# Strided attention heads: a multiplicative mask on GpSimd in place of mask products on TensorE

## The chip, the cores and the metric

The kernel runs on one core of a Trainium2 chip. Its metric is the device time of one execution, in microseconds, as the median of repeated runs. A core has five engines with a queue each: TensorE (PE in the profile; PEld is its weight load), VectorE (DVE), ScalarE (ACT), GpSimd (POOL) and SyncE (SP), which here issues most DMAs. Each queue is worked off in its own order; semaphores tie the queues to one another.

## The reference

Attention with 8 batches, 8 heads, 576 positions and head size 64, in float32, followed by a mixture of experts with one expert per token. Heads 0 to 3 look back at most 31 positions (local), heads 4 to 7 at positions that are equal modulo 32 (strided):

```python
scores = scale * np.matmul(q, k.transpose(0, 1, 3, 2))
rel = pos[:, None] - pos[None, :]
mask_local = (rel >= 0) & (rel < stride)
mask_strided = (rel >= 0) & (pos[None, :] % stride == pos[:, None] % stride)
scores = np.where(masks[None, :, :, :], scores, -1000000000.0)
attn = np.exp(scores - np.max(scores, axis=-1, keepdims=True))
attn = attn / (np.sum(attn, axis=-1, keepdims=True) + 1e-09)
x = np.matmul(attn, v)          # heads are then joined to rows of 512
```

The mixture takes the gate logits of each row, picks an expert by the largest logit (or keeps the expert of the row before, where a second gate says so), and multiplies the row's softmax probability with `relu(x @ w1[e]) @ w2[e]`; 8 experts, 512 to 1024 to 512.

## The kernel before

**Tiling.** Heads are worked in pairs: per batch pairs 0 and 1 are local, pairs 2 and 3 strided, so a strided pair stands in steps 2 and 3 of every four. A pair consists of two units (`g` 0 and 1). For strided heads the positions are regrouped by their residue modulo 32: seven residues of 18 positions make a block of 126 (`GK`), and the last four residues a block of 72 (`GL`). A strided unit has two blocks of 126 (252 columns a head), or two of 126 and one of 72 (324 columns). Inside a block only positions of the same residue, and no later ones, may be seen, so the mask is the same for every block, `maskS`.

**One unit.** `scores` writes the scores, keys on partitions and queries along the row, into a PSUM tile (two of them), and ScalarE takes the exponential into a tile `e` in SBUF (four of them) without a maximum. For local units `mask` multiplies `e` by ones and zeros on VectorE (L263). For strided units `mask` does nothing: there `scores` first writes the mask into PSUM by a product of the identity with `maskS` (bfloat16, 0 or a large negative number; L246, one for each head), and the score products (L252) are added to it, so that the exponential of what must not be seen is zero. `values` (L276) multiplies `e` with the values, which have a column of ones at the end that yields the sums; `norm` divides by them (L289, L290) on VectorE. In the profile one float32 product of L252 or L276 stands as four records.

**The order of the work** is written out by hand, in program order for each engine, in the loop at the end of `attention`. Step n, out of 35, does in this order: the load of pair n+4 (L164, L168, by SP); scores and masks of pair n; the stores of pair n-2 (L301, L307, by SP: two DMAs for a batch's local half, ten for its strided half); the transpositions of pair n-2 (L317, copied out by ScalarE, L321); values and norm of pair n-1; two steps of the weight sums of expert 0 on VectorE from step 9 on (L703; the weights themselves are loaded in step 6); after a batch's last pair the gate logits (L336) and gates (L354 onward). Local pairs of batch 0 are steps 0 and 1, its strided pairs steps 2 and 3, those of batch 1 steps 6 and 7, and so on to 30 and 31.

**What hangs on the steps.** A table `also` puts the routing into them: in step 2 `router.constants` (a row of iotas on GpSimd, L478 to L504, that VectorE reads, and a DMA from GpSimd's queue, L505); in steps 19 to 23 the routing of the first four batches on VectorE and TensorE; in steps 24 to 33 two scatters each from GpSimd's queue (L577; each writes up to 128 entries of 8 bytes to a table of slots in DRAM); in step 29, behind its two scatters, two gathers from GpSimd (L737) of the rows of the first expert tile, whose row numbers VectorE makes late in that step (L632 to L637). Before the loop, GpSimd and VectorE make `maskL` (L185 to L190) and `maskS` (L195 to L215). After the loop the experts run, on TensorE mainly (L807, L843), with the routing of the last four batches, its twenty scatters and their fetch among their first products.

Of the kernel before, what the change touches and what calls it, by code (L numbers as in the profile page):

```python
# [8 lines left out]
F32 = mybir.dt.float32  # L9
BF16 = mybir.dt.bfloat16  # L10
I32 = mybir.dt.int32
Act = mybir.ActivationFunctionType
Alu = mybir.AluOpType
# [5 lines left out]
P = 128  # L19
B, H, S, DH = 8, 8, 576, 64  # L20
# [19 lines left out]
GK, GL = PL * GC, PL * GR  # L40
# [19 lines left out]
NEG = -8.0e9  # L60
# [17 lines left out]
def across(ap, shape):  # L78

    return ap.rearrange("a (o b) -> a o b", o=1).to_broadcast(shape)  # L80
# [62 lines left out]
def attention(ctx, tc, qkl, qks, vl, vs, wg, xd, ident, router, moe):  # L143

    nc = tc.nc
    sums, probs, codes = router.sums, router.probs, router.codes
    consts = ctx.enter_context(tc.tile_pool(name="consts", bufs=1))
# [27 lines left out]
    for _ in range(WARM):  # L175
        ps = psV.tile([P, 512], F32, name="vps")
# [1 line left out]
    wgs = consts.tile([P, DK, 32], F32, name="wgs")  # L178
    nc.scalar.dma_start(out=wgs, in_=wg.rearrange("(k p) e -> p k e", p=P))

    identb = consts.tile([P, P], BF16, name="identb")
    nc.vector.tensor_copy(identb, ident)

    maskL = consts.tile([LK, LT, LQ], F32, name="maskL")
    nc.gpsimd.memset(maskL, 1.0)  # L185
# [1 line left out]
                            pattern=[[0, LT], [-1, LQ]], channel_multiplier=1)  # L187
    nc.gpsimd.affine_select(out=maskL, in_=maskL, compare_op=Alu.is_ge, fill=0.0, base=STRIDE,
                            pattern=[[0, LT], [1, LQ]], channel_multiplier=-1)
    nc.gpsimd.memset(maskL[0:STRIDE, 0], 0.0)  # L190

    maskS = consts.tile([GK, 2 * GK + GL], BF16, name="maskS")
    for n, c in ((GK, GC), (GL, GR)):
        i = consts.tile([GK, n], I32, name=f"i{n}")
        cls = consts.tile([GK, n], F32, name=f"cls{n}")  # L195
        div = consts.tile([GK, n], F32, name=f"div{n}")
        both = []
        for mult, pattern in ((1, [[0, n]]), (0, [[1, n]])):

            nc.gpsimd.iota(i, pattern=pattern, base=0, channel_multiplier=mult)  # L200
            t = consts.tile([GK, n], F32, name=f"cls{n}{mult}")
            nc.vector.tensor_copy(t, i)
            nc.vector.tensor_scalar(i, i, 65536 // c + 1, None, Alu.mult)
            nc.vector.tensor_scalar(i, i, 16, None, Alu.arith_shift_right)
            nc.vector.tensor_copy(div, i)
            nc.vector.scalar_tensor_tensor(t, div, -float(c), t, Alu.mult, Alu.add)
            both.append(t)
        nc.vector.tensor_tensor(cls, both[0], both[1], op=Alu.not_equal)
        nc.vector.tensor_scalar(cls, cls, NEG, None, Alu.mult)
        nc.gpsimd.affine_select(out=cls, in_=cls, compare_op=Alu.is_ge, fill=NEG, base=0, pattern=[[1, n]],  # L210
                                channel_multiplier=-1)
        if n == GK:
            nc.vector.tensor_copy(maskS[:, 0:2 * n].rearrange("p (a x) -> p a x", a=2), across(cls, [n, 2, n]))
        else:
            nc.vector.tensor_copy(maskS[:, 2 * GK:], cls)  # L215
# [13 lines left out]
    start = consts.tile([P, CH], F32, name="start")  # L229
    nc.vector.tensor_scalar(start, pos8, float(E), None, Alu.is_equal)  # L230

    def spans(u):

        if u.local:
            return [(3 * u.g + i, LQ, i * LQ) for i in range(3)]
        return [(j, GK if j < GT - 1 else GL, i * GK) for i, j in enumerate(range(2 * u.g, 2 + 3 * u.g))]

    def scores(u):
        t = st["qk", u.b, u.pair]
        kb, width = (LK, LQ) if u.local else (GK, GK)  # L240
        ps = psS.tile([P, 2, 512], F32, name="sps")
        sp = spans(u)
        n = sp[-1][2] + sp[-1][1]
        if not u.local:
            for h in range(2):
                nc.tensor.matmul(ps[0:GK, h, 0:n], lhsT=identb[0:GK, 0:GK],  # L246
                                 rhs=maskS[:, 0:n], start=True, stop=False, skip_group_check=True)
        for j, w, c in sp:
            m = kb if u.local else w
            for h in range(2):  # L250
                r = slice(h * DH, (h + 1) * DH)
                nc.tensor.matmul(ps[0:m, h, c:c + w], lhsT=t[r, S + j * width:S + j * width + m],  # L252
                                 rhs=t[r, j * width:j * width + w],
                                 start=(u.local and c == 0), stop=True, skip_group_check=True)
        e = work.tile([P, 2, 2 * GK + GL], F32, name="e")
        nc.scalar.activation(e[0:kb, :, 0:n], ps[0:kb, :, 0:n], Act.Exp, bias=0.0, scale=1.0 / DH ** 0.5)  # L256
        u.e = e

    def mask(u):
        if u.local:  # L260
            ev = u.e[:, :, 0:3 * LQ]
            m = maskL[:, 3 * u.g:3 * u.g + 3].rearrange("p a x -> p (a x)")
            nc.vector.tensor_tensor(ev, ev, m.rearrange("p (o x) -> p o x", o=1).to_broadcast([LK, 2, 3 * LQ]),  # L263
                                    op=Alu.mult)

    def values(u):

# [130 lines left out]
    n = PAIRS * RB + 3  # L398
# [4 lines left out]
    m = n  # L403
# [10 lines left out]
    for n in range(len(units) + 3):  # L414
        if n < len(units):
            if n + ahead < len(order):
                load(*order[n + ahead])
            if n == 6:
                steps = moe.W[0].ready(nc, w1=moe.w1, w2=moe.w2, e=0)
            for u in units[n]:  # L420
                scores(u)
                mask(u)
# [1046 lines left out]
```

## Time and profile before

| | us |
|---|---|
| median of 13 runs (742.17 to 751.01) | 744.66 |
| profiled execution | 747.47 |
| its span, from first to last instruction | 745.7 |
| TensorE busy | 697.9 |
| VectorE busy | 380.6 |
| ScalarE busy | 199.1 |
| GpSimd busy | 134.3 |
| mean granted TensorE clock | 0.953 of full speed |

The attention stage fills the first 202 us; the first expert product (L807) starts at 201.9. In the profile a row of a timeline has the start in us, the duration in us, the engine, the line, the operation, `out<-in`, partitions x elements and type, a count, and in brackets how long the engine had idled and what ended that. "issue" is time in which an engine waited for nothing that the profile shows, and "remote" a release that it can't assign. A busy TensorE is not the same as one at its peak.

### The profile page before, as it was taken

To read this page: it belongs to the slowest core of one execution; us is meant where nothing else is said; L and a number is where in the kernel's file an instruction comes from. 1 tells how busy PE (TensorE), PEld (TensorE's weight loads), DVE (VectorE), ACT (ScalarE), POOL (GpSimd) and SP (SyncE) were. 2 spreads that over 40 slices of the span, in tenths; PEclk is the share of its full clock that TensorE was granted. 3 is DMA by queue.
4 is the path that set the end of the run, shared out by engine and by line. 5 is a ranking of instruction groups with operands and counts; after the bars stand their busy time and mean duration, and the time that the engine had idled before them with its cause. 6 is when DMAs were issued, how large, how long until landed. Compare 5 with 4: busy or idle time off the path is not lost.

```text
span 745.7 us, 15189 instructions
## 1 busy us (share of the span) xinstructions
PE 697.9 (94%) x6170; PEld 623.8 (84%) x6170; DVE 380.6 (51%) x896; ACT 199.1 (27%) x360; POOL 134.3 (18%) x150
## 2 busy tenths in 40 slices
PE   8999999497899599999999999999999999999993
PEld 5887888385699589899998899999999999989992
DVE  6568756272466434473563266366346646324341
ACT  2444443041321112222212222212222222212310
POOL 3000001405127331211121120131012112111001
PEclk8999999597699799999999999999999999999997
DMA  9898778342360023604322612520071342010100
GB/s 326 262 332 289 271 276 295 125 144 62 87 226 30 3 85 103 213 30 151 127 73 78 220 58 82 204 86 31 27 247 58 125 158 73 32 35 31 31 29 27
DMA packets 38057, 95.83 MB, mean 129 GB/s; under 512 B 5358, under 2 KB 14574, under 8 KB 37888
## 3 DMA queue, kind: packets, MB, share of 16 engines
q1 hardware_dynamic: 29616, 73.77, 28.4%
q0 software_dynamic: 7744, 20.08, 8.3%
q8 instruction: 64, 1.05, 0.6%
q14 instruction: 105, 0.86, 0.3%
q10 hardware_dynamic: 528, 0.07, 0.1%
HBM read 74.93 MB, written 20.02 MB: 127 GB/s over the span
## 4 chain that ended last, share of the span: by engine, by line
PE 88%; DVE 3%; another core or an unknown queue 3%; issue 2%; DMA 1%; ACT 1%; POOL 1%; POOLq 0%; ACTq 0%
PE lps L807 31%; PE mps L843 30%; PE vps L276 6%; PE sps L252 6%; PE tps L317 4%; PE xps L750 2%; PE lps L898 2%; PE mps L909 2%; PE sps L246 2%; PE vps L354 1%; PE tps L336 1%; DMA qk<-in_qks_dram 1%; DVE xl L290 1%; DMA x<-xd,gi 0%
## 5 line engine op out<-in xcount | busy, mean ns | idle before, releaser
L807 PE MATMUL lps<-tt,ws 128*128 128x128 f32 x912 | 108.5, 275 | 1.5 <-issue 1.5
L807 PEld LDWEIGHTS lps<-tt,ws 128*128 128x128 f32 x912 | 105.0, 192 | 1.6 <-issue 1.6
L763 POOL DMA_INDIRECT out_dram<-y,tab x40 | 45.9, 1146 | 330.9 <-DVE y L795 274.5
L843 PE MATMUL mps<-wt,k 128*128 128x256 f32 x456 | 101.6, 379 | 0.0
L843 PEld LDWEIGHTS mps<-wt,k 128*128 128x128 f32 x456 | 86.6, 190 | 11.8
L795 DVE TENSOR_TENSOR h<-lps,u 128x512 f32<-128x512 f32 x57 | 39.4, 691 | 81.1 <-PE lps L807 71.0
L807 PE MATMUL lps<-xt,w1t 128*128 128x128 f32 x608 | 75.6, 278 | 0.4 <-ACT p L814 0.4
L807 PEld LDWEIGHTS lps<-xt,w1t 128*128 128x128 f32 x608 | 73.6, 195 | 2.4 <-issue 1.0
L843 PE MATMUL mps<-w2t,h 128*128 128x256 f32 x304 | 72.7, 382 | 0.0
L577 POOL DMA_INDIRECT slots<-tok,idx x40 | 41.0, 1025 | 149.9 <-DVE tok L568 138.3
L252 PE MATMUL sps<-qk 64*128 64x96 f32 (+2 forms) x704 | 57.4, 294 | 6.8 <-issue 5.6
L843 PEld LDWEIGHTS mps<-w2t,h 128*128 128x128 f32 x304 | 57.0, 193 | 7.1
L252 PEld LDWEIGHTS sps<-qk 64*128 64x128 f32 (+2 forms) x704 | 47.8, 194 | 17.0 <-issue 14.4
L737 POOL DMA_INDIRECT x<-xd,gi x40 | 39.5, 988 | 112.5 <-DVE tab L637 29.3
L794 ACT ACTIVATE h<-h 128x512 f32<-128x512 f32 x57 | 35.9, 630 | 89.1 <-DVE h L795 84.1
L256 ACT ACTIVATE e<-sps 128x576 f32<-128x576 f32 (+1 forms) x64 | 41.4, 651 | 60.2 <-PE sps L252 42.6
L807 PE MATMUL lps<-xt,ws 128*128 128x128 f32 x304 | 39.0, 284 | 6.8 <-DVE h L795 6.8
L807 PEld LDWEIGHTS lps<-xt,ws 128*128 128x128 f32 x304 | 37.1, 199 | 7.0 <-DVE h L795 6.9
L795 DVE TENSOR_TENSOR u<-lps,p 128x512 f32<-128x512 f32 x19 | 13.1, 692 | 56.8 <-PE lps L807 43.4
L794 ACT ACTIVATE h<-lps 128x512 f32<-128x512 f32 x23 | 13.7, 597 | 94.1 <-PE lps L807 69.3
L807 PE MATMUL lps<-tt,w1t 128*128 128x128 f32 x304 | 37.8, 276 | 0.9 <-issue 0.9
L289 DVE RECIPROCAL sums<-vps 128x6 f32<-128x6 f32 (+1 forms) x64 | 12.1, 188 | 51.1 <-PE vps L276 29.6
(214 smaller groups left out, 943.1 us busy)
## 6 DMA issues: line engine op xcount, KB each, us to landing
w1t<-in_w_dram SPq DMA_DIRECT2D x8, 2048.0 KB
w2t<-in_w_dram SPq DMA_DIRECT2D x8, 2048.0 KB
qk<-in_qkl_dram SPq DMA_DIRECT2D x16, 592.0 KB
qk<-in_qks_dram SPq DMA_DIRECT2D x16, 576.0 KB
vl<-in_vf_dram SPq DMA_DIRECT2D x8, 780.0 KB
vs<-in_vg_dram SPq DMA_DIRECT2D x8, 639.8 KB
xd<-xl SPq DMA_DIRECT2D x16, 288.0 KB
xd<-xs SPq DMA_DIRECT2D x64, 63.0 KB
```

Source lines behind the costliest of these rows:

```text
L246: nc.tensor.matmul(ps[0:GK, h, 0:n], lhsT=identb[0:GK, 0:GK], rhs=maskS[:, 0:n], start=True, stop=False, skip_group_check=True)
L252: nc.tensor.matmul(ps[0:m, h, c:c + w], lhsT=t[r, S + j * width:S + j * width + m], rhs=t[r, j * width:j * width + w], start=(u.local and ...
L256: nc.scalar.activation(e[0:kb, :, 0:n], ps[0:kb, :, 0:n], Act.Exp, bias=0.0, scale=1.0 / DH ** 0.5)
L276: nc.tensor.matmul(ps[a * HALF:(a + 1) * HALF, h, i], lhsT=u.e[0:m, h, q0:q0 + HALF], rhs=vt[0:m, j, 2 * i2 + h], start=(i == 0 and h == 0 ...
L317: nc.tensor.transpose(ps[:, t], src[:, t], ident)
L577: s = self.nc.gpsimd.indirect_dma_start(out=self.T, out_offset=bass.IndirectOffsetOnAxis(ap=self.idx[0:m, t, b:b + 1], axis=0), in_=self.t ...
L737: self.nc.gpsimd.indirect_dma_start(out=r.x[:, i], out_offset=None, in_=self.xd[0:r.rows], in_offset=bass.IndirectOffsetOnAxis(ap=r.gi[i], ...
L763: s = self.nc.gpsimd.indirect_dma_start(out=self.out, out_offset=bass.IndirectOffsetOnAxis(ap=r.si[i], axis=0), in_=y[:, i], in_offset=Non ...
L794: relu = lambda o, i: nc.scalar.activation(o, i, Act.Relu)
L795: add = lambda o, i, p: nc.vector.tensor_tensor(o, p, i, op=Alu.add)
L807: nc.tensor.matmul(ps[:, f], lhsT=m[:, kk, f * P:(f + 1) * P], rhs=v[:, kk], start=(start and f == 0 and kk == 0), stop=(kk == 1), skip_gr ...
L843: nc.tensor.matmul(ps[:, 0:256], lhsT=m[:, f], rhs=v[:, f], start=(start and f == 0), stop=(f == 3), skip_group_check=True)
```

## The change

The mask products and the identity in bfloat16 go. `maskS` becomes a float32 tile of ones and zeros (same residue, not later). ScalarE takes the exponential of the bare scores; for the unit with three blocks in two instructions, because the last block has 72 rows only. Then GpSimd multiplies `e` by the mask, in one instruction of 126 rows by 504 elements for the blocks of 126 of each unit, and one of 72 rows by 144 for the last block; `values` reads the result. In GpSimd's queue these stand where `mask` is called in the step, that is ahead of what `also` puts into the same step. Local heads are as before.

```diff
-    identb = consts.tile([P, P], BF16, name="identb")
-    nc.vector.tensor_copy(identb, ident)
...
-    maskS = consts.tile([GK, 2 * GK + GL], BF16, name="maskS")
+    maskS = consts.tile([GK, 2 * GK + GL], F32, name="maskS")
...
-        nc.vector.tensor_tensor(cls, both[0], both[1], op=Alu.not_equal)
-        nc.vector.tensor_scalar(cls, cls, NEG, None, Alu.mult)
-        nc.gpsimd.affine_select(out=cls, in_=cls, compare_op=Alu.is_ge, fill=NEG, base=0, pattern=[[1, n]],
+        nc.vector.tensor_tensor(cls, both[0], both[1], op=Alu.is_equal)
+        nc.gpsimd.affine_select(out=cls, in_=cls, compare_op=Alu.is_ge, fill=0.0, base=0, pattern=[[1, n]],
                                 channel_multiplier=-1)
...
-        if not u.local:
-            for h in range(2):
-                nc.tensor.matmul(ps[0:GK, h, 0:n], lhsT=identb[0:GK, 0:GK],
-                                 rhs=maskS[:, 0:n], start=True, stop=False, skip_group_check=True)
...
-                                 start=(u.local and c == 0), stop=True, skip_group_check=True)
+                                 start=(c == 0), stop=True, skip_group_check=True)
         e = work.tile([P, 2, 2 * GK + GL], F32, name="e")
-        nc.scalar.activation(e[0:kb, :, 0:n], ps[0:kb, :, 0:n], Act.Exp, bias=0.0, scale=1.0 / DH ** 0.5)
+        u.parts = [(kb, 0, n)] if u.local or not u.g else [(GK, 0, 2 * GK), (GL, 2 * GK, n)]
+        for m, a, z in u.parts:
+            nc.scalar.activation(e[0:m, :, a:z], ps[0:m, :, a:z], Act.Exp, bias=0.0, scale=1.0 / DH ** 0.5)
...
     def mask(u):
...
+            return
+        for m, a, z in u.parts:
+            ev = u.e[0:m, :, a:z]
+            nc.gpsimd.tensor_tensor(ev, ev, across(maskS[0:m, a:z], [m, 2, z - a]), op=Alu.mult)
```

## The prediction

> **What bounds the kernel now.** I read first the page's chain of work that ended last, then the same chain restricted to the attention stage (the first 202 us), then the timeline around the places where that chain leaves TensorE, then the groups by form for durations.
>
> The page: TensorE holds 88% of the chain, and the mask products (L246) are on it.
> ```profile
> span 745.7 us, 15189 instructions
> PE 88%; DVE 3%; another core or an unknown queue 3%; issue 2%; DMA 1%; ACT 1%; POOL 1%; POOLq 0%; ACTq 0%
> ```
> The chain between 0 and 100 us; columns are start, duration, what. The reader sees one schedule step on strided heads (step 7): two bursts of L246, each followed by the score products, then a transposition, the previous step's value products, the next step's scores. Nothing but TensorE. At 66.46 the chain leaves it for a load.
> ```profile
> 40.27 0.36 PE sps L246 x2
> 40.63 0.64 PE sps L252 x8
> 41.26 0.42 PE sps L246 x2
> 41.68 0.77 PE sps L252 x12
> 42.45 0.81 PE tps L317 x6
> 43.25 1.31 PE vps L276 x40
> 44.57 1.51 PE sps L252 x24
> ...
> 66.46 6.35 DMA qk<-in_qks_dram
> ```
> The timeline gives, for that step, the two exponentials, the value products that need them, and the wait at the load; further on, GpSimd's first scatter, VectorE and ScalarE coming back after long waits, and GpSimd's gather and the scatter behind it.
> ```profile
> 41.31 0.59 ACT L256 ACTIVATE e<-sps 126x504 f32<-126x504 f32 x1 [0.29 <-PE sps L252]
> 42.49 0.71 ACT L256 ACTIVATE e<-sps 126x648 f32<-126x648 f32 x1 [0.59 <-PE sps L252]
> 46.71 1.39 PE L276 MATMUL vps<-vs,e 126*64 126x65 f32 x40
> 72.85 0.71 PE L252 MATMUL sps<-qk 64*126 64x126 f32 x8 [0.78 <-DMA qk<-in_qks_dram]
> 127.52 1.04 POOL L577 DMA_INDIRECT slots<-tok,idx  x1 [113.53 <-DVE tok L568]
> 142.22 0.20 DVE L289 RECIPROCAL sums<-vps 128x6 f32<-128x6 f32 x1 [11.24 <-remote]
> 145.21 1.19 ACT L256 ACTIVATE e<-sps 128x576 f32<-128x576 f32 x2 [16.41 <-PE tps L317]
> 171.84 1.00 POOL L737 DMA_INDIRECT x<-xd,gi  x1 [29.31 <-DVE tab L637]
> 174.42 1.01 POOL L577 DMA_INDIRECT slots<-tok,idx  x1 [0.31 <-issue]
> 184.06 0.20 DVE L289 RECIPROCAL sums<-vps 128x6 f32<-128x6 f32 x1 [7.83 <-remote]
> ```
> Twice a run of scatters on GpSimd (twelve from 127.52, eight from 174.42, one each 1.28 us) goes with a TensorE whose records become ragged and with engines that wait until the run is over. In the first run TensorE is regular for 2.8 us (to 130.3) and then does until 145.0 what elsewhere takes 2.2 us. GpSimd is otherwise idle: 6.9 us busy before 127.
>
> **The change, part by part.** The profiled execution took 747.47 us (span 745.7), 0.4% over the median 744.66; I sum in microseconds and take the sum off the median.
>
> *1. Mask products removed.* 64 records of L246 (per strided step 2 of 0.36 us and 2 of 0.42 us together, so 0.78 us with the clock full) on sixteen steps. On the chain: step 2 at low clock 0.61+0.73 = 1.34; steps 3, 6, 7, 10, 11, 14, 15, 18, 19 at 0.78 = 7.0; step 22 not on it (VectorE's routing work is the chain at 112 to 117); step 23 0.36+0.73 = 1.09; 26 0.53+0.42 = 0.95; 27 and 30 0.78 each; 31 0.61+0.73 = 1.34. Sum 13.3 us. What is late next: (a) the load at 72.85. The DMA engines are 102% busy from 40 to 60 and SP spends 52.57 to 66.36 on ten stores ahead of this load, so it can move earlier only by what was won before the weight loads (issued at 38.55). Steps 6, 7, 10, 11 (4 x 0.78 = 3.1 us) may all turn into waiting. Bounds 0 and 3.1; 0.78 us of wait already stands there, so I take 3.1. (b) Steps 30 and 31 (2.1 us) I count in part 4, where GpSimd decides. Left: 13.3 - 3.1 - 2.1 = 8.1 us gained.
>
> *2. Constants.* The identity's cast (0.71) lay beside GpSimd's mask work. Two multiplications by the big negative number (0.24 and 0.21) were on the chain to the first local mask at 11.65, with their gaps 0.5 us gained.
>
> *3. Mask multiplications added.* Per strided step three on GpSimd: two of 126x504 and one of 72x144. No row of before has a two-input operation there. Nearest rows: affine select 126x126 0.29 us, 128x576 0.70 us, so 0.91 ns an element over 0.17 us. One input at this rate: 0.63 us for 504. Twice the rate for two inputs: 1.1 us, and 0.44 us for 144. Four times the rate as the far end: 2.0 us. I take 1.1, since two streams are read. So 2.6 us a step, 42 us in all. Step 7's cover, from the start of its scores: first exponential done at 1.27 (0.68 + 0.59), first mask at 2.4, second exponential (now 126x504, 0.59, and 72x144, some 0.28 by the 128x72 copy's 0.23) long done, second mask 3.5, third 3.9. The value products need unit one after 0.64+0.77+0.81+1.31+1.51+0.70 = 5.75 us and unit two 0.65 later, 6.4. Spare: 3.4 and 2.5 us, so no cost; the cover ends where the 504 operation takes over 2.2 us (1.27 + 2.29T + 0.12 = 6.4). ScalarE pays 0.16 us a step and is a quarter busy. In program order GpSimd's router constants and the table's DMA (L505) now stand behind step 2's masks: these finish at about 18.6, the iotas (1.2 us in all) by 20, and VectorE reads them only after the norm that now ends near 20; step 3's masks queue behind that DMA (1.14 us) and are done by 24.3, needed at 25.4. No cost, 1 us if the estimates slip.
>
> The Trainium skill speaks against this placement. "GPSIMD Engine Reference", section "Performance versus the Vector engine", calls GpSimd the wrong place for ordinary elementwise work, with 4497 ns for 2048 fp32 elements; by proportion 1.1 us for 504 is its estimate, and the sum would not change against the 0.63 us of the one-input row, since both are covered. "SBUF — State Buffer", section "Who interferes with whom", says that a VectorE instruction with two SBUF inputs and a GpSimd instruction that reads SBUF block each other whole; no row here shows it, and by it each of the weight sums (L703) that meets a mask would be up to 1.1 us late, on an engine that is half idle.
>
> *4. Scatters and gather now share GpSimd's queue with the masks.* In program order the first run of twelve becomes four, then step 26's masks, two, step 27's masks, six; after the gather the eight become step 30's masks, two, step 31's masks, six. First run: lost before 15.3 - 2.8 = 12.5 us. If each run is harmless for its first 2.8 us, the new ones lose 2.3, 0 and 4.9: 5.3 us gained. Ends: 0 (each scatter costs the same wherever it stands) and 12.5. Second run: gather at 171.84, then masks of step 30 from 174.1 to 177.0, two scatters to 179.5, masks of step 31 to 182.3, so the last value products end near 182.9 (TensorE, free at 177.9, waits some 3.7 us for GpSimd) and not at 192.4; six scatters behind them cost again 4.9: 9.5 - 4.9 = 4.6 us gained. Ends: 9.5 gained; and 3 lost, if all the slowness stays and the masks' wait comes on top. The third run (218 to 249, unchanged) left TensorE regular for over 20 us, so length alone doesn't set the start of the slowness. Hence I take half of each: 2.7 + 2.3 = 5.0.
>
> Sum: 8.1 + 0.5 + 5.0 = 13.6 us. 744.66 - 13.6 = 731.
>
> **The rivals.**
> B. *No relief at the scatters.* Part 4 gives 0 and, at the tail, 3 lost: 8.1 + 0.5 - 3 = 5.6, so 739. For it: the third run's behaviour follows no simple length.
> C. *GpSimd becomes the bound (slower).* The place is the wait of the value products for the third mask. It decides from 504 elements at about 2.4 us: each step is then over 0.5 us late, and 16 of these eat the 8.6. At 3.0 us the step is 1.9 us late, 30 us in all: 744.66 + 30 - 8.6 = 766. For it: no two-input row, a broadcast operand, and an unseen effect of GpSimd on its neighbours in the scatter runs. Against: the 0.91 ns an element, which would have to rise fourfold.
> D. *The stage is fed, not computed.* Each batch's SP stores and loads set the step, so the removed products turn into waits for qk loads everywhere as at 72.85; only steps 2 and 3, 22 on and the constants count: 1 to 3 us, 742. For it: the DMA share, 0.7 to 1.0 up to 130 us. Against: a single such wait on TensorE, 0.78 us.
>
> **How the numbers follow.** My forecast 0.56, B 0.20, C 0.13, D 0.11. Its own range is 723 (part 4 in full, no loss at the load) to 737. The 8 in 10: below 720 part 4's far ends would both have to hold (0.06); above 744 lies C (0.13): 720 to 744. A measurement of this kernel can tell some 0.5% from no change, 740.9 to 748.4. Faster: nearly all of the forecast, most of B, little of D: 0.77. Same: most of D, the edge of B: 0.10. Slower: C, 0.13.
>
> **What will show it.** Right: no L246; strided steps 0.78 us shorter on the chain; GpSimd rows of 126x504 near 1.1 us that nobody waits for before 125 us; a longer wait for qk near 70 us; shorter remote waits of VectorE behind the scatters; a wait of the last value products for GpSimd. Wrong: value products waiting for e on GpSimd in every strided step (C), waits for qk in every batch (D), or the same ragged 12 and 10 us at the scatters (B).

## The result, and the profile after

| | before | after |
|---|---|---|
| median, us | 744.49 (740.08 to 751.81) | 753.2 (747.21 to 757.43) |
| ratio | | 1.0103, 95% interval 1.0079 to 1.0126 |
| profiled execution, its span | 747.47, 745.7 | 752.23, 750.4 |
| VectorE busy | 380.6 | 397.5 |
| GpSimd busy | 134.3 | 183.6 |
| TensorE busy | 697.9 | 687.1 |

The change made the kernel 1.0% slower. The forecast was 731 us, 1.8% faster, with a range of 720 to 744: wrong in sign, and the time lies outside the range. TensorE's work fell by 10.8 us, as was meant, and the kernel took longer with less work.

The page of after: the span, and the chain by engine.
```profile
span 750.4 us, 15189 instructions
PE 81%; DVE 6%; another core or an unknown queue 4%; DMA 3%; issue 2%; ACT 2%; POOL 1%; SPq 0%; DVEq 0%; POOLq 0%; ACTq 0%
```
TensorE holds 81% of the chain instead of 88%; VectorE's share doubled to 6%.

How far each trace has come, as a table (the "turn" is the first transposition of a step, the first expert product is where the attention stage ends):

| us | before | after | gained |
|---|---|---|---|
| turn of step 3 | 23.63 | 18.49 | 5.1 |
| turn of step 5 | 30.79 | 30.96 | -0.2 |
| turn of step 20 | 105.22 | 104.72 | 0.5 |
| first expert product | 201.94 | 201.65 | 0.3 |
| from there to the end of the span | 543.76 | 548.75 | -5.0 |

So four things have to be explained: the first 5 us, won and lost at once; strided steps that are then hardly shorter; a late attention stage without the relief; and 5 us lost in the expert stage, which the change doesn't touch. The traced executions differ by 4.7 us and the medians by 8.7, since before's trace was 3.0 us above its median and after's 1.0 below.

**The start.** Rows of VectorE, GpSimd and TensorE of after, around 20 us. Columns of a timeline are start, duration, engine, line, operation, `out<-in`, shape, count, and in brackets the idle time before and what ended it.
```profile
19.62 3.32 DVE L495 COPY tok<-ids 128x40 int32<-128x40 int32 x1
23.78 0.42 DVE L289 TENSOR_TENSOR xs<-vps,sums 128x256 f32<-128x256 f32 x1
```
```profile
19.24 1.15 POOL L504 DMA_DIRECT2D slots<-tab  x1 [0.31 <-POOL tab L503]
20.40 2.92 POOL L263 TENSOR_TENSOR e<-e,maskS 126x504 f32<-126x504 f32 x3
```
```profile
24.35 1.51 PE L316 MATMUL tps<-ident,xs 128*128 128x128 f32 x5 [2.15 <-DVE sums L288]
```
The same copy before:
```profile
23.64 0.17 DVE L496 COPY tok<-ids 128x40 int32<-128x40 int32 x1
```
A copy that took 0.17 us takes 3.32. It ends at 22.94, which is about when the second of step 3's masks ends (20.40 and twice 1.27). Its first 0.78 us lie beside GpSimd's DMA of the router's table (the row of L504), the rest beside the two masks. In every trace with such a hold, of this copy or of a cast behind it (after, e1, e4, e5, e9, e14, e16), this DMA stands ahead of the masks, so it is not shown that masks alone hold a copy that long. Behind it in VectorE's queue stands the norm of `xs`, and TensorE, at the turn, waits 2.15 us for that. The stretches of the same time (length, TensorE busy, weight loads, VectorE, ScalarE, GpSimd, granted clock, DMA share, GB/s) show what it costs:
```profile
22.20:24.30 2.10, 0.00 (x0) 0.00 (x0) 2.07 (x8) 0.73 (x2) 1.13 (x2) 0.92 1.01 317
24.30:34.30 10.00, 9.95 (x114) 8.68 (x116) 5.20 (x12) 2.70 (x6) 0.00 (x0) 0.50 0.77 285
```
After the stop TensorE is granted half its clock for 10 us, by estimate some 5 us of work. But the lead of 5.1 us was itself in part clock, since this trace of before had its half clock earlier:
```profile
15.00:20.00 5.00, 5.00 (x38) 3.88 (x39) 0.67 (x3) 1.69 (x3) 0.00 (x0) 0.50 1.00 386
```
In two further pairs of traces (e6 and e5, e13 and e14, below) the lead at step 3 is 2.4 us, the stop is 2.2 us again, and the half clock behind it lasts 3.4 us. What all three pairs share is the place at step 6's turn: after is behind by 1.5, 1.6 and 1.3 us.

**VectorE beside GpSimd.** Groups of the page by form, the same two operations of the gates before and after, and GpSimd's masks:
```profile
L377 DVE TENSOR_SCALAR gsm<-gsm 128x5 f32<-128x5 f32 x8 | 1.4, 172 | 0.3
L379 DVE TENSOR_TENSOR probs<-ex,gsm 128x40 f32<-128x40 f32 x8 | 1.6, 200 | 0.3
```
```profile
L376 DVE TENSOR_SCALAR gsm<-gsm 128x5 f32<-128x5 f32 x8 | 5.7, 713 | 0.3
L378 DVE TENSOR_TENSOR probs<-ex,gsm 128x40 f32<-128x40 f32 x8 | 5.5, 690 | 0.3
L263 POOL TENSOR_TENSOR e<-e,maskS 126x504 f32<-126x504 f32 x32 | 39.8, 1268 | 86.6 <-ACT e L251 81.8 <-DVE code L371 4.8
L263 POOL TENSOR_TENSOR e<-e,maskS 72x144 f32<-72x144 f32 x16 | 9.3, 584 | 0.0
```
Work of 0.2 us takes 0.7 on average. The masks themselves came near the estimate (1.27 and 0.58 us against 1.1 and 0.44). Operations that read PSUM, such as the norm (0.56 us), did not stretch. The Trainium skill's page "SBUF — State Buffer", section "Who interferes with whom", has the rule: VectorE's second port pair is GpSimd's, and whoever has it shuts the other out for the whole instruction. It names copies, casts and `tensor_scalar` in their two-port modes as well as operations with two SBUF inputs, and the rows above are of these kinds. Not every such operation stretched: the weight sums (L702, two SBUF inputs), on which the prediction had put the price, kept their 0.68 us, also the two that met a mask.

**The strided steps.** Before, in the step behind a batch's logits, the turn followed the scores at once (step 6, TensorE's timeline):
```profile
34.14 0.43 PE L246 MATMUL sps<-maskS,identb 126*126 126x252 bf16 x2
34.50 0.71 PE L252 MATMUL sps<-qk 64*126 64x126 f32 x8
35.13 0.49 PE L246 MATMUL sps<-maskS,identb 126*126 126x324 bf16 x2
35.55 0.83 PE L252 MATMUL sps<-qk 64*126 64x126 f32 x12
36.32 0.87 PE L317 MATMUL tps<-ident,xl 128*128 128x128 f32 x6
```
After:
```profile
35.77 1.27 PE L245 MATMUL sps<-qk 64*126 64x126 f32 x20
37.80 0.84 PE L316 MATMUL tps<-ident,xl 128*128 128x128 f32 x6 [0.75 <-DVE lT L343]
```
`turn_x` and `logits` share the one buffer of `psT`. The mask products had covered the four copies that empty it (two on ScalarE, two on VectorE); now TensorE waits for the last, 0.75 us, about what the removed products took.

**The expert stage.** TensorE's timeline, the stops of over 1 us for which the profile has no releaser; before, then after:
```profile
300.74 2.17 PE L807 MATMUL lps<-tt,ws 128*128 128x128 f32 x18 [1.50 <-issue]
```
```profile
351.17 0.49 PE L806 MATMUL lps<-xt,w1t 128*128 128x128 f32 x3 [2.23 <-issue]
471.71 3.06 PE L806 MATMUL lps<-tt,ws 128*128 128x128 f32 x25 [1.32 <-issue]
```
Two stops, at other places, in place of one. The longer one is followed by a lower clock (stretches as above):
```profile
349.00:351.10 2.10, 0.00 (x0) 0.00 (x0) 0.00 (x0) 0.00 (x0) 0.69 (x1) 1.00 0.95 314
351.10:354.60 3.50, 3.43 (x19) 3.43 (x19) 0.00 (x0) 0.58 (x1) 0.00 (x0) 0.58 0.99 327
```

### The profile page after: what moved, and what is told of

Its sections match the earlier page's. It is cut to its first block, busy times and chain, and to the rows that moved or that the text cites. A ratio compares the mean times of both kernels' runs of the same rounds, so it can differ in the third digit from the quotient of the medians.

```text
span 750.4 us, 15189 instructions
## 1 busy us (share of the span) xinstructions
PE 687.1 (92%) x6106; PEld 619.5 (83%) x6106; DVE 397.5 (53%) x893; ACT 198.5 (26%) x376; POOL 183.6 (24%) x198
## 4 chain that ended last, share of the span: by engine, by line
PE 81%; DVE 6%; another core or an unknown queue 4%; DMA 3%; issue 2%; ACT 2%; POOL 1%; SPq 0%; DVEq 0%; POOLq 0%; ACTq 0%
PE lps L806 32%; PE mps L842 30%; PE vps L275 5%; PE sps L245 3%; PE tps L316 3%; PE xps L749 2%; PE lps L897 2%; PE mps L908 2%; DMA qk<-in_qkl_dram 2%; PE vps L353 1%; DVE xl L289 1%; PE tps L335 1%; DMA vs<-in_vg_dram 1%; ACT lT L341 1%
## 5 line engine op out<-in xcount | busy, mean ns | idle before, releaser
L806 PE MATMUL lps<-tt,ws 128*128 128x128 f32 x912 | 111.0, 278 | 2.1 <-issue 2.1
L806 PEld LDWEIGHTS lps<-tt,ws 128*128 128x128 f32 x912 | 106.9, 194 | 2.9 <-issue 2.8
L263 POOL TENSOR_TENSOR e<-e,maskS 126x504 f32<-126x504 f32 (+1 forms) x48 | 48.5, 1040 | 86.6 <-ACT e L251 81.8
L251 ACT ACTIVATE e<-sps 128x576 f32<-128x576 f32 (+2 forms) x80 | 41.1, 551 | 50.0 <-PE sps L245 31.8
L245 PE MATMUL sps<-qk 64*128 64x96 f32 (+2 forms) x704 | 50.9, 290 | 2.0 <-issue 1.9
L245 PEld LDWEIGHTS sps<-qk 64*128 64x128 f32 (+2 forms) x704 | 45.0, 196 | 5.4 <-issue 3.3
L794 DVE TENSOR_TENSOR u<-lps,p 128x512 f32<-128x512 f32 x19 | 13.1, 692 | 58.0 <-PE lps L806 42.9
```

The costliest lines, as they stand in the source:

```text
L251: nc.scalar.activation(e[0:m, :, a:z], ps[0:m, :, a:z], Act.Exp, bias=0.0, scale=1.0 / DH ** 0.5)
L263: nc.gpsimd.tensor_tensor(ev, ev, across(maskS[0:m, a:z], [m, 2, z - a]), op=Alu.mult)
L794: add = lambda o, i, p: nc.vector.tensor_tensor(o, p, i, op=Alu.add)
L806: nc.tensor.matmul(ps[:, f], lhsT=m[:, kk, f * P:(f + 1) * P], rhs=v[:, kk], start=(start and f == 0 and kk == 0), stop=(kk == 1), skip_gr ...
```

## The experiments

The runs went to several chips: e1 to e4 to one, e5 to e8 to another, e9 to e16 to a third, e17 to a fourth. The kernel before takes 743 to 745 us on each but that of e1 to e4, where it takes 708.9; the traces of e1 to e4 put no engine's idle time down to a remote release, and there is no trace of before or of the unaltered after from that chip. So a ratio is always to the kernel before on the same chip, and stages are compared within one chip where a microsecond matters. The stages of all traces, in us:

| run | ratio to before (95%) | first expert product | from there to the end |
|---|---|---|---|
| e1 after, TensorE stream padded at the start | 1.0222 (1.0185 to 1.0259) | 182.5 | 537.9 |
| e2 after, no strided mask | 1.0304 (other expert work) | 163.9 | 563.3 |
| e3 after, masks on VectorE | 1.0080 (1.0051 to 1.0109) | 170.9 | 537.8 |
| e4 before, and ones on GpSimd | 1.0234 (1.0185 to 1.0282) | 184.8 | 541.6 |
| e5 after again | 1.0106 (1.0059 to 1.0154) | 200.1 | 546.0 |
| e6 before again | | 197.3 | 541.9 |
| e7 GpSimd masks in batches 0 to 4 | 0.9989 (0.9956 to 1.0022) | 198.9 | 541.9 |
| e8 VectorE masks in batches 0 to 4 | 0.9949 (0.9921 to 0.9978) | 193.8 | 543.9 |
| e9 after, padded late | 1.0067 (1.0030 to 1.0104) | 204.1 | 544.9 |
| e10 e8, turn behind values | 1.0001 (0.9966 to 1.0036) | 201.6 | 542.9 |
| e11 after, constants early | 1.0059 (1.0025 to 1.0092) | 198.1 | 550.2 |
| e12 e10, late product constants | 0.9982 (0.9955 to 1.0010) | 198.0 | 544.2 |
| e13 before, third trace | | 204.3 | 543.0 |
| e14 after, third trace | 1.0077 (1.0047 to 1.0108) | 199.6 | 548.0 |
| e15 GpSimd masks in batches 5 to 7 | 1.0024 (0.9994 to 1.0053) | 200.1 | 542.6 |
| e16 after, scatters behind the masks | 1.0218 (1.0181 to 1.0256) | 207.7 | 550.0 |
| e17 e8, late product constants | 0.9973 (0.9945 to 1.0002) | 196.0 | 544.8 |

### Does GpSimd's work hold VectorE up? (e2, e3, e4)

e2 drops the whole mask step, so the strided mask is missing from the computation; tokens then go to other experts (42 output scatters instead of 40), and only its attention stage can be read.
```diff
-        for m, a, z in u.parts:
-            ev = u.e[0:m, :, a:z]
-            nc.gpsimd.tensor_tensor(ev, ev, across(maskS[0:m, a:z], [m, 2, z - a]), op=Alu.mult)
```


> The changed kernel without any multiplication of the strided exponentials: the strided mask is left out of the computation; the products stay removed, GpSimd has no masks. Theory B (GpSimd's multiplications hold VectorE up): VectorE's copy of the token numbers at 19.6 us takes 0.2 us and not 3.3, the gate rows of 128x5 and 128x40 fall from 0.7 to 0.2 us, TensorE does not stop at 22 us, the turn of step 6 starts near 32 us and not at 37.8, and the whole is 5 to 8 us under the changed kernel, 745 to 748. Rival T (what eats the gain is the turn's wait for the logits' copies, for which the mask products had been the cover; GpSimd is harmless): 752 to 753. Both theories leave the waits of the turn for the copies of the logits, some 0.75 us in seven batches.

e3 moves it:
```diff
-            nc.gpsimd.tensor_tensor(ev, ev, across(maskS[0:m, a:z], [m, 2, z - a]), op=Alu.mult)
+            nc.vector.tensor_tensor(ev, ev, across(maskS[0:m, a:z], [m, 2, z - a]), op=Alu.mult)
```


> The changed kernel with the mask multiplications on VectorE: by its row of 128x576 (0.75 us) 0.66 us for 504 and some 0.24 for 144, 1.56 us more of VectorE work in each strided step, 25 us in all. Theory B (GpSimd's multiplications hold VectorE up): as without any mask, within 2 us: 745 to 750, and no stop of TensorE at 22 us. Rival V (it is the multiplication itself that is on the path, whichever engine does it): 753 or more.

e4 adds to the kernel before a multiplication by ones:
```diff
+        for m, a, z in [(GK, 0, 2 * GK), (GL, 2 * GK, 2 * GK + GL)][0:1 + u.g]:
+            ev = u.e[0:m, :, a:z]
+            nc.gpsimd.tensor_tensor(ev, ev, across(ones[0:m, a:z], [m, 2, z - a]), op=Alu.mult)
```


> The kernel before, mask products kept, and beside them GpSimd multiplies the strided exponentials by ones: the added half of the change alone. Theory B (GpSimd's multiplications hold VectorE up): VectorE's copy of the token numbers takes over 3 us, its busy time rises from 381 to some 397 us, the attention stage ends 3 to 8 us later and the time is 748 to 753. Rival T (GpSimd is harmless): 744 to 746. Its TensorE program is within 12 instructions of the one before, so the expert stage should take 543 to 545 us if the place of the fetches decides it.

GpSimd is not harmless: e4, which does the added half alone, is 2.3% slower than before, twice or more of what was expected of it. The groups by form of e3 and then of e4 show VectorE without and with GpSimd's masks:
```profile
L378 DVE TENSOR_TENSOR probs<-ex,gsm 128x40 f32<-128x40 f32 x8 | 1.6, 200 | 0.3
L535 DVE TENSOR_TENSOR_SCAN cum<-run 32x576 f32<-32x576 f32 x2 | 2.7, 1346 | 0.1
L495 DVE COPY tok<-ids 128x40 int32<-128x40 int32 x1 | 0.2, 174 | 0.0
```
```profile
L385 DVE TENSOR_TENSOR probs<-ex,gsm 128x40 f32<-128x40 f32 x8 | 5.6, 704 | 0.3
L542 DVE TENSOR_TENSOR_SCAN cum<-run 32x576 f32<-32x576 f32 x2 | 3.6, 1820 | 0.1
L502 DVE COPY tok<-ids 128x40 int32<-128x40 int32 x1 | 3.2, 3204 | 0.0
```
The copy of the token numbers and the gates' rows are those of theory B; the scan, which it had not named, stretched too. Without GpSimd's masks the lead of the start lasts: the turn of step 6 came at 32.4 us in e2 and 32.6 in e3, and that of step 20 at 98.2 and 97.2, against 105.9 in e4, which also keeps the mask products. From there to the first expert product it took 65.7 us without masks, 73.7 with masks on VectorE, and with GpSimd's 78.6 in e1 (the changed kernel but for its start) and 78.9 in e4. That second stretch holds the router's scans, gates and one-hot rows, all on VectorE, so a mask on VectorE costs there too, and on GpSimd costs more. The expected 745 to 750 us of e3 would be a ratio of 1.001 to 1.007; it came out just above, at 1.008, and took 8 us more than no mask between step 20 and the first expert product: for the late part rival V has a share. Of e4's 2.3%, 3.7 us (541.6 against 537.9 in e1) lie behind the first expert product, where it has a stop of 2.21 us; nothing in the added half does anything there.

### Early or late? (e5 to e8, e13 to e15)

e7 and e8 keep the mask products in the last three batches and multiply in the first five, on GpSimd or on VectorE; e15 is the complement of e7.
```diff
+        u.times = not u.local and u.b < 5
-        if not u.local:
+        if not u.local and not u.times:
             for h in range(2):
                 nc.tensor.matmul(ps[0:GK, h, 0:n], lhsT=identb[0:GK, 0:GK],
...
+        elif u.times:
+            for m, a, z in u.parts:
+                ev = u.e[0:m, :, a:z]
+                nc.gpsimd.tensor_tensor(ev, ev, across(maskT[0:m, a:z], [m, 2, z - a]), op=Alu.mult)
```


> The changed kernel, unaltered, beside the next three: the chip of the first four runs gave 708.9 us for the kernel before, where the chip of the prediction gave 744.5, so the change has to be timed and traced beside its parts. Theory B (GpSimd's multiplications hold VectorE up, on either chip): slower than the kernel before by 1.0 to 2.5%, the whole loss after 105 us. Theory S (the result belongs to the ragged scatter runs of the first chip): where the scatters are not ragged, the removed products pay and it is 0.5% faster or more.

> The kernel before, unaltered, for a trace of the same chip. If the scatter runs were ragged by the chip alone, the scatters at 127 to 142 and 174 to 184 us leave TensorE regular here, and the first expert product comes near 168 us and not at 202.

> The change in the first five batches alone (ten of sixteen strided steps, all before the router's work); the other three batches keep their mask products. Theory B says where the loss lies: VectorE is not the chain in the first five batches, so the start's 5 us lead is lost to the stop near 20 us, the other steps come out even, and what the late masks cost (scans, gates, one-hot rows, the scatters' queue, some 10 to 15 us) is not paid: 0.995 to 1.005 of the kernel before. Rival (the loss is spread over all strided steps, by the turn's waits for the logits' copies): two thirds of the changed kernel's loss stays.

> As the run before, but with the masks of the first five batches on VectorE, mask products in the last three. In the run with all masks on VectorE, step 20 was reached 8.0 us ahead of the kernel before and all of it was lost after 105 us, where VectorE's routing work is the chain. Theory B: the 8 us stay, 0.985 to 0.992 of the kernel before: faster than both. Rival (a lead at 105 us is lost at the waits for the stores' buffers and the router whatever is done there): 0.997 to 1.005.

> The kernel before, unaltered, for the stages of this chip: first expert product at 197 to 202 us where the scatter runs leave TensorE ragged (time near 744), near 168 us where they don't (near 709).

> The changed kernel, unaltered, beside the next two. On a chip with ragged scatter runs 1.008 to 1.013 of the kernel before, as on two chips so far. On a chip without them the relief of part 4 has nothing to relieve, and by the run of ones on GpSimd (1.0234) less the removed products the ratio is 1.012 to 1.020.

> The complement of the run with GpSimd's masks in the first five batches (0.9989 on a chip with ragged runs): mask products there, GpSimd's masks in the last three. If early and late parts add up, what the changed kernel loses is all here: 1.008 to 1.014 of the kernel before with ragged runs (1.012 to 1.020 without), at or above the changed kernel. If the loss is spread over all masks: half of the changed kernel's loss, 1.004 to 1.007.

The two repeats gave chips with ragged scatter runs, and e5 and e14 the slowdown again, 1.0106 and 1.0077; theory S was not tried by the unaltered kernel. The nearest is e1, on the chip without the waits for remote releases: 1.0222, some 16 us slower, of which its late start explains some 4 to 5 (first turn at 20.04 us instead of 14.66 to 16.18 in after, e5 and e14), and that speaks against S. The early half of the change comes out even (0.9989), as expected. So does the late half, nearly (1.0024): that it holds the whole loss is refuted; for half of the loss it came out below the expected 1.004, but its interval reaches 1.0053. Early and late together make 0.1 to 0.2%; the changed kernel's 0.8 to 1.1% has another part that neither half has. The table shows it: e7 and e15 spend 541.9 and 542.6 us behind the first expert product, like the kernel before, and e5 and e14 546.0 and 548.0. In three pairs of traces the attention stage of before ended at 201.9, 197.3 and 204.3, and of after at 201.7, 200.1 and 199.6: the means, 201.2 and 200.5, don't differ beyond their scatter. The rest took 543.8, 541.9, 543.0 before and 548.7, 546.0, 548.0 after: 4.1 to 5.0 us more, each time.

With the masks on VectorE and only where it has room (e8), the change gains: 0.9949, the first expert product 3.5 us earlier than in e6. That 8 us would stay was too much; its lead at step 20 is 3.9 us (99.4 against 103.3 in e6). The 8 us had been taken between two chips (e3's 97.2 against 105.2 in the first trace of before). On the same chip e7 came to step 20 at 103.6: GpSimd's masks instead of VectorE's cost 4.3 us up to there, 3.5 of them before step 6 (37.0 against 33.5).

### Why is the untouched stage slower? (e1, e9)

The change removed 102 records from TensorE's program ahead of the expert stage (5357 to 5255 in the traces, counting each weight load, product and wait; the whole program goes from 12637 to 12535). Both runs put that many back into the changed kernel.
```diff
-    for _ in range(WARM):
-        nc.tensor.matmul(ps, lhsT=warm[:, 0:P], rhs=warm, start=True, stop=True)
+    for _ in range(65):
+        nc.tensor.matmul(ps[:, 0:110], lhsT=warm[:, 0:P], rhs=warm[:, 0:110], start=True, stop=True)
```


> The changed kernel whose 14 warm-up products of 512 columns at the start are cut into 65 of 110 columns: 102 more TensorE instructions stand ahead of the expert stage, which is what the change took away, and nothing else is different. Theory P (4.8 us of the loss lie in the expert stage, because the shorter TensorE program puts an instruction fetch at another place of it, the 2.2 us stop at 349 us first): the stage from the first expert product to the end falls from 548.7 to 544 us (543.8 in the kernel before), no such stop at 349 us, time near 748.4, ratio to before near 1.005. Rival Q (the stage is slower because of the state in which the attention stage leaves the queues or buffers): 548 to 549 us as in the changed kernel, time 753, ratio 1.010.

e9 instead, ahead of the last batch's gates:
```diff
+                if n == len(units) + 2:
+                    for _ in range(51):
+                        ps = psV.tile([P, 512], F32, name="vps")
+                        nc.tensor.matmul(ps[:, 0:8], lhsT=warm[:, 0:P], rhs=warm[:, 0:8], start=True, stop=True)
```


> The changed kernel with 51 products of 8 columns ahead of the last batch's gates, where TensorE waits 4.6 to 7 us for the last logits: 103 more TensorE instructions ahead of the expert stage than the changed kernel has (the change took 102 away), and next to no time. The changed kernel stopped twice in that stage in both traces, waiting for nothing that the profile shows (1.8 and 2.2 us ahead of a group of 3 products near 350 us, 0.7 and 1.3 us ahead of one of 25 near 470 us), the kernel before once (1.5 us ahead of one of 18 near 297 us), and its first expert product to the end is 4.1 to 5.0 us shorter. Theory P (the stops sit at fixed places of the instruction stream): one stop, ahead of a group of 18, and a ratio to before some 0.005 under the changed kernel's 1.0106, so 1.004 to 1.007. Rival Q (they depend on the time or on the data moved): two stops as before, 1.010.

TensorE's timeline of e1, and of e9, the stops of over 1 us without a releaser behind 260 us:
```profile
276.17 2.17 PE L806 MATMUL lps<-tt,ws 128*128 128x128 f32 x18 [1.28 <-issue]
```
```profile
304.00 2.27 PE L810 MATMUL lps<-tt,ws 128*128 128x128 f32 x18 [1.55 <-issue]
```
In both, the one stop is back ahead of a group of 18 products, where all three traces of before have it, and the two others are gone. All traces with the changed kernel's TensorE program (after, e5, e14, and e11 and e16, which only move other work) stop ahead of the same group of 3 and the same group of 25 (the second for 0.68 us only in e5 and e14). So the place in theory P stands: the stops belong to places in TensorE's instruction stream, on each chip, and the change moved them. Two runs that were made for another purpose show how fixed the places are. e3's program has 12 records fewer ahead of the stage than after's, and its three stops stand six products (a product and its weight load are two records) further on in the work; e4's has 12 more than before's, and its stop stands six products earlier. Counted from the program's start, the stop comes at record 6564 or 6565 in before, e1, e4, e6, e9 and e13, and at 7148 or 7149 and again at 8796 in after, e3, e5, e11, e14 and e16.

The stage's own times agree. All traces but e2's run the same 3531 products there, and between the places of the stops they take the same time in every trace (42.9 us from the first place to the second, 103.0 from the second to the third). The four stretches that hold the places (of 60, 120, 120 and 80 products) take 48.6, 48.0 and 47.6 us together in the three traces of before, 52.6, 49.6 and 52.1 in those of after (after, e5, e14), and with the padding 48.4 in e9 and 47.6 in e1. So the padding brought this time back, and of the 4.1 to 5.0 us between before and after 1.6 to 4.5 lie at the stops.

The times of the whole kernels don't decide it. e9's ratio is 1.0067, within its expectation, but e14 on the same chip has 1.0077, and the padding was not free: the small products took 5.5 us, and the first expert product came at 204.1 us (e14: 199.6), while the rest took 544.9 (e14: 548.0). e1's time says little: its warm-up products take longer, and the first turn comes at 20.04 us instead of 14.66; nor is there a trace of after on its chip, and e3, with the shorter program, spent the same 538 us (in the four stretches 50.2 us against e1's 47.6, ahead of them 2.7 us less). What the shorter program costs differs from trace to trace: e3 has two stops of 1.2 and 1.1 us, after one of 2.2 with 3.5 us of low clock behind it. That these are instruction fetches is likely (two packets of the instruction queue move in the 2.1 us of after's long stop, while the DMA engines are busy for 95% of it) but was not tried by itself; nor is it known why other places of the stream show no stop.

### The start (e11)

```diff
-    also[2] = [router.constants]
+    also[1] = [router.constants]
```


> The changed kernel with the router's constants issued at the end of step 1, ahead of step 2's masks in GpSimd's queue, instead of at the end of step 2. Theory C (the 5 us lost between steps 3 and 6 come from VectorE's copies of these constants, which meet step 3's masks, and the half clock that follows TensorE's stop of 2.2 us): no stop at 22 us, step 6's turn 3 to 5 us earlier than 36.4 us, and 1.004 to 1.007 of the kernel before where the changed one has 1.0106. Rival (the copies only meet step 2's masks instead): 1.009 to 1.012.

The copies now run between step 2's masks (14.84 to 17.80 us) and step 3's (from 18.71), this one in 0.17 us, and TensorE goes on (timeline of e11):
```profile
18.34 0.17 DVE L495 COPY tok<-ids 128x40 int32<-128x40 int32 x1
```
```profile
23.63 0.77 PE L316 MATMUL tps<-ident,xs 128*128 128x128 f32 x5
```
There is no stop of 2 us at 22 us, only one of 1.16 that ends at 19.72 (as step 3's turn waits for a norm); the clock stays at 1.00 up to 45 us, and step 6's turn comes at 32.7 us; in e14, on the same chip, at 36.1. So theory C has the place and the size of that loss. But the lead of 3.4 us is down to 1.2 at step 20 (101.3 against 102.5). The row that takes most of it, of e11:
```profile
70.77 1.40 PE L245 MATMUL sps<-qk 64*126 64x126 f32 x20 [2.87 <-DMA qk<-in_qks_dram]
```
That is the load of step 14 which the prediction had named: with the start in order TensorE reaches it too early. 1.0059 lies within the expectation, but beside e14's 1.0077 on the same chip the gain is within the intervals; the trace, not the time, shows the cause. Two more stops of the expert stage were longer here (2.53 and 0.94 us), which ate the rest.

### The turn's wait (e10, e12, e17)

```diff
+        late = n == len(units) or (n > 4 and n < len(units) and order[n - 2][1] == 0)
-        if 0 <= n - 2 < len(units) and n != len(units):
+        if 0 <= n - 2 < len(units) and not late:
             turn_x(*order[n - 2])
...
-        if n == len(units):
+        if late:
             turn_x(*order[n - 2])
```


> The run with the masks of the first five batches on VectorE (0.9949 of the kernel before), and in the step behind each batch's logits the turn of the x columns is put behind the value products instead of ahead of them. Theory T (without mask products the turn stands where the logits' copies still hold the one PSUM buffer that it needs; 0.85 to 1.4 us of TensorE's waiting in each of five batches): these waits go, and 4 to 5 us with them: 0.988 to 0.991. Rival (the step is set by the loads or by VectorE, the wait only moves): 0.993 to 0.996.

> The second run of these four, with the constants of the mask products (the identity's cast and the bf16 mask of large negative numbers) made in step 5 instead of at the start. In the traces the first turn came at 17.06 us with them at the start and at 16.18 without. If this lead of 0.9 us lasts: 0.001 under the second run, so 0.987 to 0.990. If the start is set by the first loads: the same as the second run.

> The run with the masks of the first five batches on VectorE (0.9949 of the kernel before), and the constants of the remaining mask products made in step 5 instead of at the start; the turn stays ahead of the values. Between the two runs with the turn moved, the later constants were worth 0.0019 of the time. If that adds up: 0.991 to 0.994. If the start is set by the first loads: 0.994 to 0.996.

The waits for the logits' copies went, and the time rose from 0.9949 to 1.0001. TensorE's timeline of e10 shows why:
```profile
36.38 1.36 PE L363 MATMUL vps<-fold,lT 128*128 128x9 f32 x12 [1.10 <-DVE sums L298]
37.67 2.31 PE L255 MATMUL sps<-qk 64*126 64x126 f32 x20
```
The gates now wait for VectorE's norms of the values that have moved next to them, and the scores behind take 2.31 us instead of 1.27, at a granted clock of 0.50. So the theory that this order would give the wait back is refuted: the wait moves on. Other orders were not tried. Late constants gave 0.2% between e10 and e12, within their intervals, and e17 (0.9973) can't be told from e8 (0.9949). Both versions are ahead of the changed kernel; only e8 is clearly ahead of the kernel before.

### The scatters (e16)

```diff
-        also[m + i // 2].append(do)
+        also[len(units)].append(do)
```


> The changed kernel with all twenty of the first scatters issued in step 32, behind the last masks, instead of two a step from step 25. The gather in step 30 no longer stands behind them, nor do the masks of steps 26, 27, 30 and 31. Theory V (the late loss is VectorE held up by GpSimd's masks: scans, gates, one-hot rows): the attention stage keeps that loss of some 6 us, and on a chip with ragged runs gains what these cost, the first expert product 10 us or more earlier, 0.98 to 1.00 of the kernel before; without ragged runs it gains only the masks' waits behind the scatters, 3 to 5 us, and stays 1.005 to 1.015. Theory G (the late loss is the shared GpSimd queue alone): faster than the kernel before on either chip, 0.99 or less. Ends: the next run of scatters starts in the expert stage at 215 us, and twenty more scatters of 1.28 us take 26 us ahead of it: if they delay it, up to 10 us come back.

Without scatters the late attention stage is fast: step 32's turn comes at 172.8 us, 11.4 earlier than in e14. Then TensorE and ScalarE stand still; e16's timeline of TensorE:
```profile
190.94 1.33 PE L316 MATMUL tps<-ident,xs 128*128 128x128 f32 x5 [17.36 <-remote]
201.46 1.91 PE L335 MATMUL tps<-xT,wgs 128*32 128x504 f32 x8 [8.35 <-ACT xT L320]
```
17.36 and 8.35 are 25.7 us, and twenty scatters of 1.28 us are 25.6. The first expert product is 8 us later than in e14, 1.0218 in all. Both theories expected a gain on this chip, and both fell: here twenty scatters in one place cost about their own duration. That they cost the same where they are spread was not measured by itself. Why the releases come late while GpSimd issues scatters, and why not on the chip of e1 to e4, stays open. The share of the shared queue in the late loss wasn't settled by this run.

## Why the prediction was wrong, step by step

- *Part 1, the products removed (8.1 us, of these 5.2 before step 20).* The removal is real: TensorE does 10.8 us less. Between the turns of steps 6 and 20 the products took 5.5 us (7 steps of 0.78); I took off 3.1 for the load of step 14, 2.3 of it for steps of this stretch, which leaves 3.1, and 2.0 were gained (68.9 us before, 66.9 after; 1.7 and 6.8 in the two other pairs of traces, where e13's granted clock was 0.91 in this stretch). The loss had another reason than the one I gave: what came next in every batch was the turn's wait for the logits' copies, 3.4 us in this stretch of after (0.73, 1.85 and 0.77), covered until then by the very products that went. The load I named bit only in e11, where the start was in order.
- *Part 2, the constants (0.5 us).* The first strided steps did come earlier, 5.1 us by step 3 together with the first products; the 0.5 was not measured by itself; the nearest to it is 1.3 us between the first turns of e10 and e12 (17.23 and 15.96), which differ in when the product's constants are made.
- *Part 3, the masks on GpSimd ("so no cost", "No cost, 1 us if the estimates slip").* The durations were near, the cover held, and in after TensorE waits for no mask before 125 us: rival C did not come. But I priced GpSimd's work by who waits for its result, and not by who shares its port. The rule stood in the text, with its price on the weight sums, and was put at nothing because VectorE is half idle on average. The weight sums did not stretch; the constants' copies, which met GpSimd's table DMA and step 3's masks, did: one of them took 3.3 us, and the stop and the half clock lost what the start had won: at step 6's turn I had 3.4 us gained (1.34, twice 0.78, 0.5), and the trace has 1.5 lost (36.32 to 37.80). In the late stage VectorE grew busier by 8.5 us. It is not the chain there, though. Of the chain's 82 us VectorE holds 8.5 instead of 4.3, ScalarE 8.7 instead of 1.9, "another core or an unknown queue" 18.6 instead of 11.2, and TensorE 44.1 instead of 59.9: the others took up TensorE's relief. The stretch from 120 to 202 us, before, then after:
```profile
120.00:202.00 82.00, 62.83 (x825) 50.09 (x823) 35.04 (x139) 25.02 (x47) 23.31 (x24) 0.77 0.41 129
```
```profile
120.00:202.00 82.00, 59.35 (x821) 49.74 (x822) 43.50 (x147) 25.17 (x53) 38.52 (x39) 0.81 0.41 128
```
- *Part 4, shorter scatter runs (5.0 us).* I took half of what a harmless first 2.8 us would give. The end at 0, "each scatter costs the same wherever it stands", is what came: behind step 20 the change gained -0.2 us in the first pair of traces where 7.8 were predicted (5.0 here, 2.8 of products), and e16 puts the cost of a scatter near its own length. Rival B had this outcome, and missed by the other terms. That the scatters' place alone brought nothing is not shown, since GpSimd's masks came into the same stretch.
- *The rest of the kernel was counted at nothing.* It cost 5.0, 4.1 and 5.0 us in the three pairs of traces, over half of the 6 to 8 us by which the change is slower (0.8 to 1.1%). Of these 4.1, 1.6 and 4.5 lie at the stops that moved with the length of TensorE's program; the rest is spread over the stage and stays open. No step of the prediction looked behind 202 us, though the one stop was in the trace of before, at 300.74.

For the first pair of traces the working closes: predicted 5.7 to step 20 (1.34 and 7.0, less 3.1, and 0.5), measured 0.5; predicted 7.8 from there to the first expert product, measured -0.2; predicted 0 behind it, measured -5.0. That makes 4.7 us more span, 745.7 to 750.4. No rival had a path to a slower kernel except through C.

## What to carry to other kernels

Price work moved to GpSimd by what VectorE does at that moment, row by row, and not by VectorE's mean load: a 0.2 us copy that met a DMA issue and two masks of GpSimd took 3.3 us, and the engine that waited behind it then ran at half its clock, for 10 us in one trace and 3.4 in two others. Before a cover is removed, look for what it covered: the products on the path were also the time in which a PSUM buffer was emptied. And compare the untouched part of the program too, product by product: a change in one stage can move stops of another, so a difference of half a per cent may belong to the layout of the instructions and not to what the change does.

## What was not expected of the hardware

- Stops of TensorE with no releaser keep their place in the instruction stream, counted from its start: one of 1.3 to 1.55 us in five traces of three kernels with 12637 or 12638 TensorE records, two or three at other places in five traces with 12535. With 12 records more or fewer (e4, e3) they stand six products earlier or later in the work.
- A stop can cost more than itself. Behind 260 us, after stops of 1.95 to 2.24 us (after, e4, e11, e14, e16) the granted clock was 0.52 to 0.66 for 3.5 us; after stops of 1.1 to 1.83 us (before, e1, e3, e5, e9) it stayed 0.95 or more. This is no clean rule: a stop of 2.53 us in e11 and one of 1.98 in e16 were followed by 1.00.
- The same kernel took 743 to 745 us on most chips here and 708.9 on one, whose four traces put no idle time down to a remote release.
